# Block-causal attention and a gated MLP on one core: the smallest weights guarded by ScalarE, on-chip transfers issued by ScalarE, and half of w2 converted after the MLP has begun

## The chip, the cores and the metric

The kernel runs on one core of a Trainium2 chip. The metric is the device time of one execution in microseconds (us), as the median of three runs. Engines are named as the profile names them: PE is the matrix engine (PEld its weight loads), DVE the vector engine, ACT the scalar engine (ScalarE), POOL is GpSimd, SP the sync engine, which in the kernel before issues every DMA (transfer).

## The reference

Eight sequences of 576 tokens pass through attention with 8 heads of 64, causal by blocks of 64 tokens, and the 4608 results of 512 features through a gated MLP:

```python
scores = scale * np.matmul(q, k.transpose(0, 1, 3, 2))      # 8 x 8 x 576 x 576
scores = np.where(block_i >= block_j, scores, -1e9)
attn = np.exp(scores - max); attn = attn / (sum(attn) + 1e-9)
x = (attn @ v) as 4608 x 512
h = ((x @ w1) * (x @ w2)) @ w3                               # 512 -> 1024 -> 1024
out = h @ w_out                                              # 1024 -> 512
```

The weights come as 64-bit floats (w1, w2, w3, w_out), so the kernel reads each as pairs of 32-bit words and makes 32-bit floats of them on the chip.

## The kernel before, in words

**The folded weights.** The kernel multiplies w3 by w_out once, at the start (eight groups of matmuls at L358, 16 instructions each, in plain 32-bit floats), so that the MLP is only x@w1, x@w2, their product, and one matmul with the folded weight. For the rest each operand is kept as a rounded high part and a low part of the remainder (`w1h`, `w1l`, `wh`, `wl` and so on), and three matmuls stand for one.

**The early stage** runs pairs 0 to 3 of heads (the whole first sequence), one pair after the other (`pair(n)`), with `EARLY_PLAN` as the order of its steps. A letter is a step: S a tile of scores with its exponentials (L230, L238), V a part of the probabilities times v (L269), M a part of the next pair's row maxima (`shift_mask`), A and B the next operands of the scores (`prep_qk`), N and T taking and normalising the result, and C one step of the generator `gen_w`, which loads weights. There are ten Cs for a pair, so 40 in all, and `gen_w` has 40 steps: 8 for w_out, 24 for w3 (two loads for each of eight groups) with the eight loads of w1 between them, and 8 for w2, in the order of w2's rows c and then of its two column halves h.

**One load of a weight** (`load_w`, 40 of them, 128 x 512 values each) is a DMA of 512 KB into one of five buffers `wraw`, then on ACT the absolute value of the upper word (L135), then on DVE four operations: a maximum with 2^-15, the guard for tiny values (L136), a shift with a mask (L137), an operation that puts the sign in (L138), and one that puts the lower word in (L141). For w1 and w2 (`load_split`) a rounded copy on ACT (L147) and a subtraction on DVE (L148) follow.

**The two on-chip transfers.** `shift` (L196) moves the row maxima of one head into a row of the score operands, and `prep_qk` (L206) copies the high parts of q and k to the other half of the partitions. Both are issued by SP, behind the loads that SP issues in the same queue.

**The main stage** runs pairs 4 to 31 with `PLAN`; its letter F is one step of the MLP of the sequences already done (`gen_moe`): 6 matmuls, and four steps make one of eight column blocks f of x@w1 and x@w2. Block f uses the columns 128f to 128f+127 of w1 and w2. In pair 4 the first three Fs are left out (`DELAY`), so that its two halves j hold 9 and 12 of these steps. The order of PE is written out by hand from here on, by the order of the program (`manual_schedule`); on the other engines a scheduler orders instructions by their place in the program (their priority) and by when it expects them to be ready.

**Memory.** The early pool (w_out, w3, `ve`, `pe`, `wraw`, `wbits`) is closed after pair 3, and the late pool (`ph`, `rsum`, `pl`, `vs`, `gh`, `gl`, and then by first use `p32`, `xlow`, `a32`, `g32`, `xh`, `xl`, `o32`) takes the same addresses. A late buffer waits for the last reader of the early one under it.

Of the kernel before, what the change touches and what calls it, by code (L numbers as in the profile page):

```python
# [16 lines left out]
P = 128  # L17
B, H, S, D = 8, 8, 576, 64
BLK = 64
# [11 lines left out]
BIG = 8.0e9  # L31

# [18 lines left out]
)  # L51

# [6 lines left out]
def block_causal_attention__then__gated_mlp_kernel(ctx, tc, qkv, consts, ident_in, w1, w2, w3t, wout, out_t):  # L59
# [47 lines left out]
    def open_early(pool):  # L107
        tl["early"] = pool
        tl["wo"] = pool.tile([P, NF, DM], F32, name="wo")

    def open_late():
# [7 lines left out]
        tl["gh"] = pool.tile([P, NF, HALF], F32R, name="gh")  # L119
        tl["gl"] = pool.tile([P, NF, HALF], F32R, name="gl")  # L120

    def load_w(dst, src, k):
# [13 lines left out]
        V.tensor_scalar(out=u, in0=u, scalar1=2.0**-15, scalar2=None, op0=ALU.max)  # L136
# [13 lines left out]
    def load_rows(dst_h, dst_l, src, c):  # L150
        for h in range(2):
# [42 lines left out]
    def shift(n, j):  # L194
        row = qk[j][oth[j].start : oth[j].start + 1, 1, :].rearrange("p (i r) -> p i r", r=BLK)
        nc.sync.dma_start(out=row.bitcast(F32), in_=ms_of[n][0:NB, j * BLK : (j + 1) * BLK].bitcast(F32))  # L196

    def prep_qk(n, j):
# [7 lines left out]
        nc.sync.dma_start(out=qk[j][x, 0::2, :].bitcast(F32), in_=high.bitcast(F32))  # L206
# [15 lines left out]
    def s_tile(n, j, parts, p_early):  # L222
# [10 lines left out]
        for c, ks, at, q0, q1 in todo:  # L233
# [7 lines left out]
            if c == 0:  # L241
                p32 = rsum[:, q0:q1]
            else:
                p32 = tl["late"].tile([P, 448], F32, tag="p32", name=f"p{n}_{j}", bufs=2)[ks, 0:w]
# [91 lines left out]
    def gen_w(wp):  # L336
# [12 lines left out]
        for m in range(NF):  # L349
            t3 = wp.tile([P, NF, P], F32, tag="w3", name="w3", bufs=2)  # L350
# [16 lines left out]
        for c in range(NC):  # L367
            yield from load_rows(w2h, w2l, w2, c)

    def gen_moe(b):  # L370
        mp, gh, gl = tl["late"], tl["gh"], tl["gl"]
        for h in range(2):
            for f in range(NF):
# [11 lines left out]
                a32 = mp.tile([P, HALF], F32, tag="a32", name="a32", bufs=2)  # L385
                nc.scalar.copy(a32, acc[0][:, 0:HALF])
                g32 = mp.tile([P, HALF], F32, tag="g32", name="g32", bufs=2)
                nc.vector.tensor_tensor(out=g32, in0=acc[1][:, 0:HALF], in1=a32, op=ALU.mult)  # L388
                nc.scalar.copy(gh[:, f, :], g32)  # L389
                nc.gpsimd.tensor_tensor(out=gl[:, f, :], in0=g32, in1=gh[:, f, :], op=ALU.subtract)  # L390
                yield
            for e in range(DM // P):
                t = ps_m.tile([P, 512], F32, tag="psm", name="o")
                es = slice(e * P, (e + 1) * P)
                for f in range(NF):
                    for s, (l, r) in enumerate(((wh, gh), (wl, gh), (wh, gl))):
                        nc.tensor.matmul(t[:, 0:HALF], l[:, f, es], r[:, f, :], start=(f == 0 and s == 0), stop=(f == NF - 1 and s == 2))  # L397
# [23 lines left out]
    def pair(n):  # L421
# [9 lines left out]
        for j in range(2):  # L431
            xps = ps_x.tile([P, 1024], F32, tag="psx", name=f"x{n}_{j}")
            p_early = wp.tile([P, 1600], F32, tag="pe", name=f"pe{n}_{j}") if early else None
# [39 lines left out]

    for n in range(NPAIR):
        pair(n)
    fill(weights, 100)
# [60 lines left out]
```

## Time and profile before

| | |
|---|---|
| median of 3 runs | 1007.41 us (1006.82 to 1007.84) |
| the profiled execution's own time | 1008.37 us |
| its span, first to last instruction | 1006.6 us |
| PE busy | 961.6 us, 96% |
| DVE busy | 718.8 us, 71% |
| ACT busy | 547.9 us, 54% |
| POOL busy | 521.1 us, 52% |

The profile is one execution, recorded by the hardware. Busy times are sums over the whole span; the early stage is the first 150 us or so of it. The main stage is long and uniform, so the shares of the whole span say little of the early one, and the rows further down are cut by stretches.

### The profile page before, as it was taken

How to read it: one execution, taken by the hardware profiler on the slowest of the kernel's cores; microseconds unless marked ns; L12 is line 12 of the kernel's file. 1: busy time of each engine (PE TensorE's matmuls, PEld its weight loads, DVE VectorE, ACT ScalarE, POOL GpSimd, SP SyncE). 2: the span in 40 equal slices, each digit the busy share in tenths (PEclk: the TensorE clock that was granted, in tenths of full speed). 3: DMA queues.
4: the chain of work that ended last, by engine and by line, in shares of the span. 5: the costliest groups of instructions: out<-in, count | busy, mean ns of one | idle time of the engine just before them, and what ended most of it. 6: DMA issues, size and time to landing. Idle time of an engine off the chain costs nothing.

```text
span 1006.6 us, 18165 instructions
## 1 busy us (share of the span) xinstructions
PE 961.6 (96%) x6594; PEld 886.1 (88%) x6624; DVE 718.8 (71%) x1356; ACT 547.9 (54%) x1433; POOL 521.1 (52%) x525
## 2 busy tenths in 40 slices
PE   4699958999999999999999999999999999999998
PEld 2354548999999999999999999999999999999998
DVE  7999997767777777777777767777777777774100
ACT  4655755555565655555555566555555655653211
POOL 0000006667665766666666657576666766573211
PEclk9799978999999999999999999999999999999999
DMA  8776522122212221221222222212212222110000
GB/s 247 240 257 195 170 82 61 55 80 61 85 57 78 61 74 38 70 73 56 78 61 85 61 74 61 84 32 67 73 58 76 61 85 61 37 24 25 1 25 24
DMA packets 36409, 80.39 MB, mean 80 GB/s; under 512 B 4384, under 2 KB 20896, under 8 KB 36320
## 3 DMA queue, kind: packets, MB, share of 16 engines
q1 hardware_dynamic: 36320, 79.23, 26.5%
q8 instruction: 52, 0.85, 0.4%
q14 instruction: 37, 0.30, 0.1%
HBM read 50.76 MB, written 9.44 MB: 60 GB/s over the span
## 4 chain that ended last, share of the span: by engine, by line
PE 60%; DVE 23%; ACT 9%; issue 6%; DMA 2%; DVEq 0%; ACTq 0%
PE ab L381 23%; PE o L397 20%; DVE pl L248 7%; PE s L230 6%; PE x L285 4%; PE mx L179 3%; DVE g L388 2%; ACT ph L246 2%; PE w L358 2%; ACT p L245 2%; DVE m L183 2%; DVE wbits L138 1%; DVE x L323 1%; DVE rb L322 1%; DVE qk L157 1%
## 5 line engine op out<-in xcount | busy, mean ns | idle before, releaser
L251 POOL TENSOR_TENSOR rsum<-rsum,p 128x448 f32<-128x448 f32 x224 | 178.3, 796 | 120.4 <-ACT p L245 113.6
L248 DVE TENSOR_TENSOR pl<-p,ph 128x448 fp32r<-128x448 f32 x168 | 150.9, 911 | 64.1 <-ACT ph L246 63.2
L389 ACT CAST gh<-g 128x288 fp32r<-128x288 f32 x128 | 55.5, 433 | 219.3 <-DVE g L388 219.3
L390 POOL TENSOR_TENSOR gl<-g,gh 128x288 fp32r<-128x288 f32 x128 | 108.3, 846 | 123.0 <-ACT gh L389 122.9
L230 PE MATMUL s<-qk 128*128 128x288 f32 (+4 forms) x768 | 160.7, 317 | 9.2 <-DMA qk<-ms 3.5
L381 PE MATMUL ab<-xh,w1h 128*128 128x288 f32 x512 | 152.0, 297 | 6.8 <-ACT xh L332 6.8
L381 PE MATMUL ab<-xh,w2h 128*128 128x288 f32 x512 | 154.1, 301 | 0.0
L397 PE MATMUL o<-gh,wh 128*128 128x288 f32 x512 | 153.4, 300 | 0.0
L381 PE MATMUL ab<-xh,w1l 128*128 128x288 f32 x512 | 151.6, 296 | 0.0
L381 PE MATMUL ab<-xl,w2h 128*128 128x288 f32 x512 | 151.5, 296 | 0.0
L381 PE MATMUL ab<-xl,w1h 128*128 128x288 f32 x512 | 151.5, 296 | 0.0
L381 PE MATMUL ab<-xh,w2l 128*128 128x288 f32 x512 | 151.4, 296 | 0.0
L397 PE MATMUL o<-gl,wh 128*128 128x288 f32 x512 | 150.8, 295 | 0.0
L397 PE MATMUL o<-gh,wl 128*128 128x288 f32 x512 | 150.8, 295 | 0.0
L207 POOL TENSOR_TENSOR qk<-raw,qk 64x1152 fp32r<-64x1152 f32 x54 | 144.3, 2672 | 2.0
L220 POOL TENSOR_TENSOR vs<-raw,vs 128x320 fp32r<-128x320 f32 x56 | 49.9, 891 | 174.2 <-ACT vs L157 174.2
L230 PEld LDWEIGHTS s<-qk 128*128 128x128 f32 (+1 forms) x768 | 116.9, 184 | 26.1 <-issue 6.1
L183 DVE TENSOR_REDUCE m<-mx 128x1 f32<-128x512 f32 (+6 forms) x320 | 128.6, 449 | 15.8 <-PE mx L179 13.2
L246 ACT ACTIVATE ph<-s 128x288 fp32r<-128x288 f32 x336 | 131.3, 392 | 0.0
L388 DVE TENSOR_TENSOR g<-ab,a 128x288 f32<-128x288 f32 x128 | 57.7, 451 | 74.4 <-PE ab L381 71.2
L245 ACT ACTIVATE p<-s 128x448 f32<-128x448 f32 x224 | 85.5, 382 | 45.8 <-PE s L230 44.2
L285 PE MATMUL x<-ph,vs 128*128 128x128 f32 x336 | 104.1, 319 | 0.0
(71 smaller groups left out, 2141.6 us busy)
## 6 DMA issues: line engine op xcount, KB each, us to landing
raw<-in_qkv SPq DMA_DIRECT2D x32, 896.0 KB
qk<-qk SPq DMA_DIRECT2D x64, 288.0 KB
out_t<-o SPq DMA_DIRECT2D x64, 144.0 KB
wraw<-in_w3t SPq DMA_DIRECT2D x16, 512.0 KB
wraw<-in_w SPq DMA_DIRECT2D x16, 512.0 KB
wraw<-in_wout SPq DMA_DIRECT2D x8, 512.0 KB
qk<-ms SPq DMA_DIRECT2D x64, 2.2 KB
cst<-in_consts SPq DMA_DIRECT2D x1, 288.0 KB
```

What stands on the lines that cost most here:

```text
L183: nc.vector.reduce_max(m[:, col : col + 1], sc, axis=AX.X)
L207: (nc.vector if n <= EARLY else nc.gpsimd).tensor_tensor(out=low, in0=rqk[o], in1=high, op=ALU.subtract)
L230: nc.tensor.matmul(t[ks, at : at + q1 - q0], qk[j][:, 2 + s, kr], qk[j][:, s, q0:q1], start=(s == 0), stop=(s == 1))
L245: nc.scalar.activation(p32, t[ks, at : at + w], AF.Exp, scale=SCALE)
L246: nc.scalar.activation(ph[ks, o : o + w], t[ks, at : at + w], AF.Exp, scale=SCALE)
L248: nc.vector.tensor_tensor(out=low, in0=p32, in1=ph[ks, o : o + w], op=ALU.subtract)
L251: nc.gpsimd.tensor_tensor(out=r, in0=r, in1=p32, op=ALU.add)
L285: nc.tensor.matmul(xps[:, to : to + w], v[:, c, :], pr[:, a : a + w], start=(u < 2 and s == 0), stop=(u in (0, len(PV) - 1) and s == len(p ...
L381: nc.tensor.matmul(t[:, 0:HALF], l[:, c, fs], r, start=(c == 0 and s == 0), stop=(c == NC - 1 and s == 2))
L388: nc.vector.tensor_tensor(out=g32, in0=acc[1][:, 0:HALF], in1=a32, op=ALU.mult)
L390: nc.gpsimd.tensor_tensor(out=gl[:, f, :], in0=g32, in1=gh[:, f, :], op=ALU.subtract)
L397: nc.tensor.matmul(t[:, 0:HALF], l[:, f, es], r[:, f, :], start=(f == 0 and s == 0), stop=(f == NF - 1 and s == 2))
```

## The change

- `load_w`: for w_out and w3 (24 of the 40 loads) the guard is not DVE's maximum any more. ACT takes the upper 16 bits of each absolute value as an unsigned integer, subtracts 0x3800 by a bias and cuts at zero (Relu), in place. For w1 and w2 (16 loads) the maximum stays. `wbits` has 5 buffers instead of 6.
- `queue(n)`: the transfers of L196 and L206 of pairs 0 to 4 are issued by ACT, later ones by SP as before.
- w2 is loaded by column halves: first the four loads of columns 0 to 511, then the four of columns 512 to 1023. The last four Cs do nothing (`LEAVE`), and those four loads follow after pair 3, still before the early pool is closed. Pair 4's first half (j = 0) takes a priority as of before these loads.
- The late buffers are laid out by hand: `p32`, `a32` and `g32` are two plain buffers each, used in turn; `gh` and `gl` are two halves each (f 0 to 3 and f 4 to 7); the early `w3` stands right behind w_out; `pe` is 2048 columns wide, of which 1600 are used as before.

```diff
 def load_w(dst, src, k):
-        u = tl["early"].tile([P, 512], F32, tag="wbits", name="wbits", bufs=6)
+        u = tl["early"].tile([P, 512], F32, tag="wbits", name="wbits", bufs=5)
...
         nc.scalar.activation(u, high.bitcast(F32), AF.Abs)
-        V.tensor_scalar(out=u, in0=u, scalar1=2.0**-15, scalar2=None, op0=ALU.max)
+        if dst is None:
+            V.tensor_scalar(out=u, in0=u, scalar1=2.0**-15, scalar2=None, op0=ALU.max)
+        else:
+            top = u.bitcast(U16).rearrange("p (c two) -> p c two", two=2)[:, :, 1]
+            nc.scalar.activation(top, top, AF.Relu, bias=floor)
...
+    def queue(n):
+        return nc.scalar if n <= EARLY else nc.sync
...
-        nc.sync.dma_start(out=row.bitcast(F32), in_=ms_of[n][...])
+        queue(n).dma_start(out=row.bitcast(F32), in_=ms_of[n][...])
...
-        nc.sync.dma_start(out=qk[j][x, 0::2, :].bitcast(F32), in_=high.bitcast(F32))
+        queue(n).dma_start(out=qk[j][x, 0::2, :].bitcast(F32), in_=high.bitcast(F32))
...
-        for c in range(NC):
-            yield from load_rows(w2h, w2l, w2, c)
+        for h in range(2):
+            for c in range(NC):
+                yield from load_rows(w2h, w2l, w2, c, [h])
...
                 if step == "C":
-                    fill(weights, 1)
+                    if left[0] > LEAVE:
+                        left[0] -= 1
+                        fill(weights, 1)
                     continue
-                with tc.high_priority(offset=0) if early else nullcontext():
+                with (
+                    tc.high_priority(offset=0) if early
+                    else tc.high_priority(offset=tc.cur_priority - left[1]) if n == NPAIR and j == 0
+                    else nullcontext()
+                ):
...
+    left = [10 * NPAIR, 0]
     for n in range(NPAIR):
         pair(n)
+    left[1] = tc.cur_priority
     fill(weights, 100)
```

## Rows read from the trace of the kernel before

**Rows 1.** Busy time by stretches of the span. Columns: the stretch and its length in us, then PE, PEld, DVE, ACT and POOL busy us with the number of instructions, then the granted PE clock (1.00 is full speed), the busy share of the DMA engines and GB/s.

```profile
17.00:41.70 24.70, 15.31 (x59) 10.07 (x59) 23.60 (x50) 16.38 (x33) 0.00 (x0) 0.89 0.80 232
41.70:125.00 83.30, 81.80 (x250) 41.98 (x254) 81.78 (x172) 50.83 (x99) 0.00 (x0) 0.97 0.67 210
125.00:138.00 13.00, 11.78 (x51) 7.71 (x51) 12.03 (x22) 8.31 (x17) 0.00 (x0) 0.87 0.44 135
138.00:153.50 15.50, 3.82 (x16) 3.07 (x14) 14.28 (x29) 6.39 (x13) 2.52 (x2) 0.64 0.09 20
153.50:167.00 13.50, 13.49 (x78) 12.96 (x80) 9.48 (x15) 6.96 (x21) 8.47 (x8) 0.78 0.31 92
167.00:181.00 14.00, 14.00 (x109) 13.63 (x108) 11.60 (x27) 9.08 (x25) 9.58 (x10) 1.00 0.10 21
181.00:211.00 30.00, 29.71 (x221) 28.79 (x221) 21.29 (x39) 17.62 (x49) 18.79 (x19) 1.00 0.29 82
...
241.00:900.00 659.00, 654.61 (x4824) 635.26 (x4847) 489.18 (x909) 379.08 (x1046) 435.01 (x430) 1.00 0.22 64
```

**Rows 2.** PE's instructions in order of time: start, length (us), line, operation, number merged, and in brackets the idle time before them and what ended it.

```profile
41.76 9.58 PE L358 MATMUL w<-wo,w 128*128 128x512 f32 x16 [4.41 <-DVE w L141]
...
61.65 7.11 PE L358 MATMUL w<-wo,w 128*128 128x512 f32 x16
...
120.39 4.45 PE L358 MATMUL w<-wo,w 128*128 128x512 f32 x10
...
137.40 0.43 PE L269 MATMUL x<-pe,ve 64*128 64x64 f32 x2
...
143.43 1.09 PE L230 MATMUL s<-qk 128*128 128x288 f32 x3 [3.50 <-DMA qk<-ms]
...
153.50 0.61 PE L381 MATMUL ab<-xh,w1h 128*128 128x288 f32 x1 [6.82 <-ACT xh L332]
...
158.90 0.44 PE L381 MATMUL ab<-xh,w1h 128*128 128x288 f32 x1
...
159.51 0.29 PE L381 MATMUL ab<-xh,w1h 128*128 128x288 f32 x1
...
176.58 0.38 PE L381 MATMUL ab<-xh,w2h 128*128 128x288 f32 x1
```

**Rows 3.** The chain of waits that ended last, 112 to 154 us: start, length (us), and what the chain consists of there.

```profile
136.01 1.16 ACT qk L157
137.19 2.90 DMA qk<-qk
140.08 0.61 ACT w2h L147
...
145.46 0.35 DVE tr L309
...
150.75 0.57 DVE w2l L148
151.32 1.35 DVE x L323
153.02 0.44 ACT xh L332
```

**Rows 4.** DVE's instructions in order of time, columns as in Rows 2.

```profile
37.87 0.42 DVE L137 TENSOR_SCALAR wbits<-wbits 128x512 int32<-128x512 int32 x1
38.20 0.42 DVE L136 TENSOR_SCALAR wbits<-wbits 128x512 f32<-128x512 f32 x1
38.54 0.69 DVE L138 SCALAR_TENSOR_TENSOR wbits<-wraw,wbits 128x512 int32<-128x512 int32 x1
39.14 0.42 DVE L137 TENSOR_SCALAR wbits<-wbits 128x512 int32<-128x512 int32 x1
...
122.32 0.75 DVE L323 TENSOR_TENSOR x<-x,rb 128x576 f32<-128x576 f32 x1
...
145.46 0.78 DVE L309 STREAM_TRANSPOSE tr<-x 64x576 f32<-64x576 f32 x1
...
147.59 0.17 DVE L310 TENSOR_SCALAR rr<-tr 64x18 f32<-64x18 f32 x1
...
149.67 0.26 DVE L320 RECIPROCAL rr<-rr 128x18 f32<-128x18 f32 x1
149.97 0.78 DVE L322 STREAM_TRANSPOSE rb<-rr 128x576 f32<-128x576 f32 x1
```

**Rows 5.** Groups of instructions of the first 155 us: line, engine, operation, shapes, number, then busy us and mean ns of one, and the idle time before them.

```profile
L136 DVE TENSOR_SCALAR wbits<-wbits 128x512 f32<-128x512 f32 x40 | 16.5, 417 | 0.3 <-ACT wbits L135 0.3
...
L147 ACT CAST w2h<-wbits 128x512 fp32r<-128x512 f32 x8 | 4.9, 617 | 6.8 <-DVE wbits L141 6.8
```

**Rows 6.** The same view, the absolute value on ACT, and beside it two of them in order of time.

```profile
L135 ACT ACTIVATE wbits<-wraw 128x512 f32<-128x512 f32 x40 | 26.9, 677 | 19.0 <-DMA wraw<-in_w3t 9.4 <-DMA wraw<-in_w 4.9 <-DMA wraw<-in_wout 2.5
...
18.37 1.25 ACT L135 ACTIVATE wbits<-wraw 128x512 f32<-128x512 f32 x2
```

**Rows 7.** The two on-chip transfers in the first 155 or 160 us, as SP issues them (shortest, median and longest time of SP for one issue, in ns), and what SP's queue waited for: us in total, times, longest.

```profile
L196 SPq DMA_DIRECT2D qk<-ms x10: 751/794/887, 17.1 to 141.7; - x10
...
L206 SPq DMA_DIRECT2D qk<-qk x10: 602/660/687, 6.5 to 137.2; - x10
...
SPq L206 <- PE s L230: 9.1, 4, 4.0
```

More of the change, by code (lines that the diff above doesn't have):

```diff
@@ L31 @@
 BIG = 8.0e9
+U16 = mybir.dt.uint16
 PC = [0, 576, 1024, 1344, 1536]
@@ L51 @@
 )
+LEAVE = 4
 DELAY = 3
@@ L109, in open_early @@
         tl["wo"] = pool.tile([P, NF, DM], F32, name="wo")
+        tl["w3"] = [pool.tile([P, NF, P], F32, name=f"w3_{i}") for i in range(2)]
     def open_late():
@@ L118, in open_late, with late_tile @@
         tl["vs"] = [pool.tile([P, 5, P], F32R, name=f"vs{j}") for j in range(2)]
-        tl["gh"] = pool.tile([P, NF, HALF], F32R, name="gh")
-        tl["gl"] = pool.tile([P, NF, HALF], F32R, name="gl")
+        tl["p32"] = [pool.tile([P, 448], F32, name=f"p32_{i}") for i in range(2)]
+        tl["a32"] = [pool.tile([P, HALF], F32, name=f"a32_{i}") for i in range(2)]
+        tl["g32"] = [pool.tile([P, HALF], F32, name=f"g32_{i}") for i in range(2)]
+        g = [[pool.tile([P, NF // 2, HALF], F32R, name=f"g{p}{i}") for p in "hl"] for i in range(2)]
+        tl["gh"], tl["gl"] = zip(*g)
+    turn = {"p32": 0, "a32": 0, "g32": 0}
+    def late_tile(name):
+        turn[name] ^= 1
+        return tl[name][turn[name]]
+    floor = cpool.tile([P, 1], F32, name="floor")
+    nc.vector.memset(floor, -float(0x3800))
     def load_w(dst, src, k):
         t = tl["early"].tile([P, 1024], F32, tag="wraw", name="wraw", bufs=5)
-        u = tl["early"].tile([P, 512], F32, tag="wbits", name="wbits", bufs=6)
+        u = tl["early"].tile([P, 512], F32, tag="wbits", name="wbits", bufs=5)
         wide = t.bitcast(I32)
@@ L148, in load_split, with load_rows @@
         nc.vector.tensor_tensor(out=dst_l, in0=val, in1=dst_h, op=ALU.subtract)
-    def load_rows(dst_h, dst_l, src, c):
-        for h in range(2):
+    def load_rows(dst_h, dst_l, src, c, hs=range(2)):
+        for h in hs:
             cs = slice(h * 512, (h + 1) * 512)
@@ L195, in shift @@
         row = qk[j][oth[j].start : oth[j].start + 1, 1, :].rearrange("p (i r) -> p i r", r=BLK)
-        nc.sync.dma_start(out=row.bitcast(F32), in_=ms_of[n][0:NB, j * BLK : (j + 1) * BLK].bitcast(F32))
+        queue(n).dma_start(out=row.bitcast(F32), in_=ms_of[n][0:NB, j * BLK : (j + 1) * BLK].bitcast(F32))
     def prep_qk(n, j):
@@ L243, in s_tile @@
             else:
-                p32 = tl["late"].tile([P, 448], F32, tag="p32", name=f"p{n}_{j}", bufs=2)[ks, 0:w]
+                p32 = late_tile("p32")[ks, 0:w]
             nc.scalar.activation(p32, t[ks, at : at + w], AF.Exp, scale=SCALE)
@@ L366, in gen_w @@
             evacuate()
-        for c in range(NC):
-            yield from load_rows(w2h, w2l, w2, c)
+        for h in range(2):
+            for c in range(NC):
+                yield from load_rows(w2h, w2l, w2, c, [h])
     def gen_moe(b):
-        mp, gh, gl = tl["late"], tl["gh"], tl["gl"]
+        mp = tl["late"]
+        gh = [tl["gh"][f // 4][:, f % 4, :] for f in range(NF)]
+        gl = [tl["gl"][f // 4][:, f % 4, :] for f in range(NF)]
         for h in range(2):
@@ L384, in gen_moe @@
                     acc.append(t)
[L385 removed]
+                a32 = late_tile("a32")
                 nc.scalar.copy(a32, acc[0][:, 0:HALF])
[L387 removed]
+                g32 = late_tile("g32")
                 nc.vector.tensor_tensor(out=g32, in0=acc[1][:, 0:HALF], in1=a32, op=ALU.mult)
[L389 to L390 removed]
+                nc.scalar.copy(gh[f], g32)
+                nc.gpsimd.tensor_tensor(out=gl[f], in0=g32, in1=gh[f], op=ALU.subtract)
                 yield
@@ L396, in gen_moe @@
                     for s, (l, r) in enumerate(((wh, gh), (wl, gh), (wh, gl))):
-                        nc.tensor.matmul(t[:, 0:HALF], l[:, f, es], r[:, f, :], start=(f == 0 and s == 0), stop=(f == NF - 1 and s == 2))
+                        nc.tensor.matmul(t[:, 0:HALF], l[:, f, es], r[f], start=(f == 0 and s == 0), stop=(f == NF - 1 and s == 2))
                     if f % 2 and f < NF - 1:
```

4 lines of the change are left out of this document (2 added, 2 removed).

## The prediction

> **What bounds the kernel now.** I read the busy time by stretches first [rows 1]. From 241 to 900 us PE is busy 654.6 of 659 us at full clock and nothing else is near that: the main stage is PE's, and the change takes no matmul away. So what can be won lies before it. There the reader should look at PE and DVE side by side. From 17 to 41.7 us DVE is busy 23.6 of 24.7 us and PE 15.3. From 41.7 to 125 us both are full: PE 81.8 and DVE 81.8 of 83.3 us. From 138 to 153.5 us DVE is busy 14.3 of 15.5 us and PE 3.8, at a clock of 0.64.
>
> Busy could mean waiting, so PE's order of time comes next [rows 2]. Sixteen L358 instructions take 7.11 us at 61.65 and ten take 4.45 at 120.39, that is 0.44 us each throughout, so PE works there at one steady rate. Two other things stand in these rows. The first group starts late, after 4.41 us of idling for DVE, and takes 9.58 us, which is the rate of the lower clock (1.2 GHz). And the last probabilities-times-v of pair 3 ends at 137.8 us, while the MLP gets its operand only at 153.5, after 6.82 us of idling.
>
> The chain of waits says what lies between: work on w2 (L147, L148), with the transpose of pair 3's result at 145.46 and its normalising at 149.97 and 151.32 strung in between [rows 3, 4]. DVE takes its instructions in a fixed order, and w2's operations stand ahead of the result. So the bounds in order are: DVE to 41.7 us, PE with DVE beside it to 125, DVE alone to 153.5, then PE.
>
> **The guard.** Durations overlap on DVE: a shift starts 0.33 us and a maximum 0.34 us before the next instruction, though each is listed at 0.42; an operation of two inputs costs 0.60 [rows 4]. I count by these distances. 24 maxima at 0.34 are 8.2 us of DVE. How many lie on the path? Ten come before the first L358 (eight loads of w_out, two of w3), 3.4 us, in the stretch where DVE is the bound. The others fall between 41.7 and 125 us, where PE is full without them, so they shorten nothing by themselves. Bounds of the first part are 0 (the DMA engines are busy 0.80 of that stretch [rows 1], so the weights may not come sooner) and 3.4 us. I take 3.4, since PE's wait named DVE and not a transfer.
>
> On ACT 24 instructions are new. The nearest row is the absolute value of the same 512 columns: 677 ns, the second of two 0.58 us after the first [rows 6], so 13.9 to 16.2 us. Bounds: all of it hidden, since ACT is busy only 75.5 of the 121 us from 17 to 138 [rows 1], or as much on the path as rival D says. I take it as hidden but for the friction below.
>
> The row says that ACT needs 677 ns where DVE needs 417 [rows 5, 6]. A rule of the Trainium skill speaks against the move: the page "ScalarE: Activation LUTs", section "Rules for kernel authors", says to use VectorE and not ScalarE for relu and max, and its section on the table load gives 280 ns + 0.833 ns per column with a bias pointer, an estimate of 707 ns and 17.0 us for the 24. The rows agree with its direction; it speaks of the price of one instruction, and by it rival D would have 0.8 us more to place.
>
> **Transfers by ACT.** SP needs 794 ns for one issue of L196 and 660 for one of L206, and there are ten of each in pairs 0 to 4 [rows 7]: 14.5 us that move to ACT's queue. No row shows an issue by ACT. The bounds are nothing and SP's own price, and I take SP's price for ACT's time. Behind a waiting issue ACT's exponentials would stand, and PE's V steps wait for these. But the copy of L206 follows ACT's own cast, which overwrites the same operands and so has waited for the same matmuls; L196 follows ACT's own product. What the transfers may win is SP's delay behind its loads, of which I take nothing. The fifth buffer instead of a sixth `wbits`, the halved `gh` and `gl` and the buffers used in turn issue nothing more; I take zero for them.
>
> **The second half of w2.** One such load costs DVE 2 x 0.34 + 3 x 0.60 = 2.48 us with its subtraction, and four cost 9.9 us. These leave the stretch before 153.5 us. Then DVE alone would be done by 153.5 - 8.2 - 9.9 = 135.4 us. PE alone: the last V ends at 137.8 - 3.4 = 134.4 us, and behind it come transpose (0.78), the sums (0.17 and 0.26), the second transpose (0.78), the product (0.75) and the cast on ACT (0.44) in a row [rows 3, 4], 3.2 us, with some 0.4 us of hand-overs: 138.0 us. So with w2 out of the way PE and this last run of short steps are late next, and PE decides. The two bounds lie only 2.6 us apart, and ACT is fuller. For the friction I take 1.5 us, what PE idles from 41.7 to 125 us where two engines are full; its bounds are 0 and 8 (the remaining tail as it is). The MLP's first operand is then there at 139.5 us instead of 153.5: **14.0 us won.**
>
> **What the second half costs later.** It is used first by block f = 4, in step 19 of pair 4's 21 MLP steps, which began at 176.58 us, 23 us after the stage began [rows 2]. DVE is busy 9.48 + 11.60 = 21.1 of pair 4's 27.5 us and 21.3 of the next 30 [rows 1], so it has 6.4 us free in pair 4, and some 1.5 us while pair 3's last run waits. 9.9 - 6.4 - 1.5 = 2.0 us don't fit and hold PE. Bounds are 0 (the 8.7 us free in the next pair take them) and 9.9. Behind these operations DVE's low parts of the probabilities are queued, and PE's V steps wait for them. `xlow` of pair 4 lies over a raw buffer of the second moved load; two loads are 5.0 us of DVE and its first half has 4.0 free, so I add nothing.
>
> **The clock.** After its idling PE runs at 1.2 GHz until about 159.2 us (0.44 us for an instruction at 158.90, 0.29 at 159.51 [rows 2]), which costs half of 5.7, so 2.9 us. It may be kept or lost a second time; I take no change, with 2.9 us on either side.
>
> **The sum.** 14.0 - 2.0 = 12.0 us less. The profiled execution's 1008.37 us (span 1006.6 and 1.8 around it) becomes 996.4. That execution is 0.96 us above the median of the runs; against 1007.41 the same step gives **995.4 us**.
>
> **Rivals.**
>
> A. The forecast, 990 to 1001 us: chance 0.60.
>
> B. More than that: DVE sets the end at 135.4 us (18.1 us), nothing spills, and PE keeps its clock (2.9 us), 21 us in all: 986 us. For it: PE's idling of 3.50 and 6.82 us before 153.5 goes. Against it: PE needs its 138.0 us. Chance 0.10, for 986 to 990 and a little below.
>
> C. The gain is hidden: the last stretch is a run of hand-overs rather than DVE's amount. Pair 4's scores wait there for a cast of 1.16 us, a transfer of 2.90 us, and L196 until 143.43 [rows 2, 3], and none of that gets shorter. If only the 3.4 us of the start and the moved operations after 145.46 on the chain (0.57 at 150.75, and some 2 us between) are won, 6 us, and 2 to 4 are given back later, the time is 1004 us, with 1001 to 1006.5 as its stretch. For it: the DMA step on the chain; against it: pair 3's result waited from 137.8 to 145.46 with nothing but w2 and the masks on DVE. Chance 0.20, of which 0.06 falls within 0.2% of the time before.
>
> D. ACT takes over as the bound (the slower side). It gets 16.2 us of guard, 14.5 of issues, and, if the 9.1 us for which SP's copies waited for PE's scores [rows 7] now stop ACT, 39.8 us; less 4 x (0.68 + 0.62) = 5.2 us moved away with w2 that is 34.6 us. Its place is ACT's queue from 17 to 138 us, where exponentials stand behind each wait. ACT has 45.5 us free there, mostly in waits that can't all be filled. From 35% on the path (12.0 of 34.6) the gain is gone; at 60% it is 20.8 us, and the time 1007.4 + 20.8 - 12.0 = 1016 us. For it: ACT's queue is in order and would be some 90% full. Against it: nothing on the chain before waits long for ACT. Chance 0.10, of which 0.02 falls within 0.2%.
>
> **How the numbers follow.** What a measurement of this kernel can tell from no change is about 0.2%, 2 us. Faster by more: A 0.60, B 0.10 and 0.14 of C, so 0.84; within: 0.06 + 0.02 = 0.08; slower: 0.08. The range is 986 to 1006 us: it holds A, B but for its lowest part and most of C, and leaves out D and the slow end of C.
>
> **What would show it.** The first L358 starts near 38 us instead of 41.76; if not, the loads held it. The first L381 that waits for `xh` starts near 139.5 us, and no w2 operation stands between pair 3's last V and its L323. ACT is 82 to 91% busy from 17 us up to there; if PE comes to wait for `pe` or `qd` by more than a few us in all, D is at work. From then to the end PE needs what it needed before, 1006.6 - 153.5 = 853.1 us, and some 2 more, with the wait in pair 4 at L285 or at block f = 4. A stage start later than 147 us, or a spill over 8 us, makes the forecast wrong.

## The result, and the profile after

The changed kernel is **slower**: 1014.98 us (median of 6 runs, 1010.75 to 1017.26) against 1007.51 (6 runs, 1004.62 to 1008.05), a ratio of 1.0076, 95% interval 1.0061 to 1.0090. The forecast was 995.4, with a range up to 1006. The profiled execution took 1017.09 us, its span is 1015.3. A profile is a single execution: this one lies 2.1 us above its kernel's median, that of the kernel before 1.0 us, so differences of a microsecond or two between profiles may be scatter.

Busy time by stretches after, with the columns of [rows 1]:

```profile
17.00:41.70 24.70, 16.95 (x56) 10.56 (x57) 20.34 (x42) 19.97 (x39) 0.00 (x0) 0.86 0.72 217
41.70:125.00 83.30, 78.14 (x243) 40.23 (x242) 74.00 (x145) 58.10 (x108) 0.00 (x0) 0.96 0.64 200
125.00:138.00 13.00, 11.46 (x42) 6.80 (x40) 12.86 (x22) 9.90 (x20) 0.00 (x0) 0.92 0.47 140
138.00:153.50 15.50, 9.48 (x38) 6.75 (x36) 14.91 (x34) 9.09 (x19) 0.00 (x0) 0.72 0.20 66
...
167.00:181.00 14.00, 13.85 (x83) 13.41 (x84) 7.61 (x16) 6.73 (x19) 5.43 (x6) 0.77 0.00 1
...
241.00:900.00 659.00, 654.86 (x4838) 636.60 (x4837) 487.32 (x904) 380.45 (x1050) 433.39 (x429) 1.00 0.23 65
```

DVE did get lighter: by 3.3 us from 17 to 41.7 and by 7.8 from there to 125. But PE got emptier beside it (78.14 us instead of 81.80 from 41.7 to 125), and from 138 to 153.5 DVE is as full as before. The stretch from 241 to 900 is what it was. So the loss lies before 181 us.

PE in order of time after (columns of [rows 2]; L384, L295, L256, L410 and L311 are L358, L269, L230, L381 and L285 of before; the first line shows 12 of the group's 16 instructions):

```profile
40.78 5.42 PE L384 MATMUL w<-wo,w 128*128 128x512 f32 x12
...
125.95 3.59 PE L384 MATMUL w<-wo,w 128*128 128x512 f32 x8
...
146.35 1.00 PE L295 MATMUL x<-pe,ve 128*128 128x192 f32 x2 [1.77 <-ACT pe L264]
148.03 0.68 PE L295 MATMUL x<-pe,ve 64*128 64x64 f32 x2 [0.67 <-ACT pe L264]
...
156.19 0.61 PE L410 MATMUL ab<-xh,w1h 128*128 128x288 f32 x1 [4.13 <-ACT xh L358]
...
157.25 1.48 PE L256 MATMUL s<-qk 128*128 128x448 f32 x4
...
167.15 0.53 PE L311 MATMUL x<-pl,vs 128*128 128x192 f32 x1 [2.81 <-DVE pl L274]
```

The fold starts 1.0 us earlier and ends 4.7 us later (129.5 instead of 124.8). Pair 3's last V ends 10.9 us later, at 148.7. The tail behind it is shorter, and the matmul that waits for the MLP's operand starts at 156.19 instead of 153.50: 2.7 us late. From there to the end PE needs 859.1 us instead of 853.1: another 6.0. The two make up the 8.7 us between the spans.

DVE in order of time after, which answers to [rows 4] (L170 is the subtraction of L148, L349 the product of L323):

```profile
150.98 0.78 DVE L335 STREAM_TRANSPOSE tr<-x 64x576 f32<-64x576 f32 x1
151.79 0.69 DVE L170 TENSOR_TENSOR w2l<-wbits,w2h 128x512 fp32r<-128x512 f32 x1
152.51 0.17 DVE L336 TENSOR_SCALAR rr<-tr 64x18 f32<-64x18 f32 x1
152.72 0.69 DVE L170 TENSOR_TENSOR w2l<-wbits,w2h 128x512 fp32r<-128x512 f32 x1
153.33 0.26 DVE L346 RECIPROCAL rr<-rr 128x18 f32<-128x18 f32 x1
153.50 0.63 DVE L170 TENSOR_TENSOR w2l<-wbits,w2h 128x512 fp32r<-128x512 f32 x1
154.05 0.77 DVE L348 STREAM_TRANSPOSE rb<-rr 128x576 f32<-128x576 f32 x1
154.92 0.76 DVE L349 TENSOR_TENSOR x<-x,rb 128x576 f32<-128x576 f32 x1
```

In after **the second half of w2 did not leave**. In the program its loads stand behind pair 3, but the last of its subtractions still run between the transpose of pair 3's result and its normalising, as before. All eight loads of w2 are done before the MLP's waiting matmul. E1, E2, E8 and E16 below show that this isn't so in every kernel with this place in the program.

The guard, in groups from 17 to 156 us (columns: operation, count, busy us, mean ns, then idle time before them and what ended it), against [rows 5, 6]:

```profile
L153 ACT ACTIVATE wbits<-wraw 128x512 f32<-128x512 f32 x37 | 24.1, 670 | 14.4 <-DMA wraw<-in_w3t 9.3 <-DMA wraw<-in_w 2.2 <-DVE wbits L163 2.1
L158 ACT ACTIVATE wbits<-wbits,floor 128x512 uint16<-128x512 uint16 x22 | 18.6, 868 | 0.2
L159 DVE TENSOR_SCALAR wbits<-wbits 128x512 int32<-128x512 int32 x38 | 15.6, 421 | 5.7 <-ACT wbits L158 5.6
```

One guard takes ACT 868 ns, and DVE's shift waits for it 5.6 us in all.

The transfers, on ACT in order of time (for [rows 7]):

```profile
145.12 0.60 ACTq L232 DMA_DIRECT2D qk<-qk  x1
...
146.12 1.59 ACTq L222 DMA_DIRECT2D qk<-ms  x2
147.76 0.22 ACT L264 ACTIVATE pe<-s 64x64 f32<-64x64 f32 x1 [1.46 <-issue]
```

Two issues of 0.8 us stand in front of the exponential for which PE's last V of pair 3 waits. In all ACT's waits for its own issues are 2.6 us from 17 to 156 us (1.5 for `pe`, 0.8 for `qd`, 0.3 for an absolute value).

### The profile page after: what moved, and what is told of

The parts are those of the page before. It is cut to its first block, busy times and chain, and to the rows that moved or that the text cites. A ratio compares the mean times of both kernels' runs of the same rounds, so it can differ in the third digit from the quotient of the medians.

```text
span 1015.3 us, 18193 instructions
## 1 busy us (share of the span) xinstructions
PE 968.0 (95%) x6624; PEld 892.5 (88%) x6624; DVE 710.8 (70%) x1333; ACT 565.1 (56%) x1457; POOL 519.7 (51%) x525
## 4 chain that ended last, share of the span: by engine, by line
PE 59%; DVE 23%; ACT 10%; issue 6%; DMA 3%; POOL 0%; DVEq 0%; ACTq 0%; POOLq 0%; SPq 0%
PE ab L410 22%; PE o L426 20%; DVE pl L274 7%; PE s L256 6%; PE x L311 4%; PE mx L205 3%; DVE g L417 3%; ACT ph L272 2%; ACT p L271 2%; DMA wraw<-in_w3t 2%; DVE x L349 2%; PE w L384 2%; DVE rb L348 1%; DVE m L209 1%; ACT xh L358 1%
## 5 line engine op out<-in xcount | busy, mean ns | idle before, releaser
L277 POOL TENSOR_TENSOR rsum<-rsum,p 128x448 f32<-128x448 f32 x224 | 177.8, 794 | 120.2 <-ACT p L271 113.5
L419 POOL TENSOR_TENSOR gl<-g,gh 128x288 fp32r<-128x288 f32 x128 | 108.4, 847 | 127.3 <-ACT gh L418 127.3
L256 PE MATMUL s<-qk 128*128 128x288 f32 (+4 forms) x768 | 162.6, 319 | 6.4 <-ACT pe L264 3.9
L410 PE MATMUL ab<-xh,w1h 128*128 128x288 f32 x512 | 152.8, 298 | 4.1 <-ACT xh L358 4.1
L410 PE MATMUL ab<-xh,w2h 128*128 128x288 f32 x512 | 155.1, 303 | 0.0
L410 PE MATMUL ab<-xl,w1h 128*128 128x288 f32 x512 | 152.6, 298 | 0.0
L410 PE MATMUL ab<-xh,w1l 128*128 128x288 f32 x512 | 152.4, 298 | 0.0
L410 PE MATMUL ab<-xh,w2l 128*128 128x288 f32 x512 | 152.3, 297 | 0.0
L410 PE MATMUL ab<-xl,w2h 128*128 128x288 f32 x512 | 152.3, 297 | 0.0
L233 POOL TENSOR_TENSOR qk<-raw,qk 64x1152 fp32r<-64x1152 f32 x54 | 144.2, 2670 | 2.0
L256 PEld LDWEIGHTS s<-qk 128*128 128x128 f32 (+1 forms) x768 | 118.4, 186 | 20.6 <-ACT pe L264 5.8
L311 PE MATMUL x<-ph,vs 128*128 128x128 f32 x336 | 104.3, 320 | 0.0
```

The source lines that it names most:

```text
L233: (nc.vector if n <= EARLY else nc.gpsimd).tensor_tensor(out=low, in0=rqk[o], in1=high, op=ALU.subtract)
L256: nc.tensor.matmul(t[ks, at : at + q1 - q0], qk[j][:, 2 + s, kr], qk[j][:, s, q0:q1], start=(s == 0), stop=(s == 1))
L277: nc.gpsimd.tensor_tensor(out=r, in0=r, in1=p32, op=ALU.add)
L311: nc.tensor.matmul(xps[:, to : to + w], v[:, c, :], pr[:, a : a + w], start=(u < 2 and s == 0), stop=(u in (0, len(PV) - 1) and s == len(p ...
L410: nc.tensor.matmul(t[:, 0:HALF], l[:, c, fs], r, start=(c == 0 and s == 0), stop=(c == NC - 1 and s == 2))
L419: nc.gpsimd.tensor_tensor(out=gl[f], in0=g32, in1=gh[f], op=ALU.subtract)
```

## The experiments

The kernel before had medians of 1006.96 to 1007.26 us beside the experiments, and the ratios are to these. "After" and "before" name the two kernels. No experiment leaves out a part of the reference.

**Undoing one part of the change**

E1, the guard back on DVE:

```diff
-        if dst is None:
-            V.tensor_scalar(out=u, in0=u, scalar1=2.0**-15, scalar2=None, op0=ALU.max)
-        else:
...
-            nc.scalar.activation(top, top, AF.Relu, bias=floor)
+        V.tensor_scalar(out=u, in0=u, scalar1=2.0**-15, scalar2=None, op0=ALU.max)
```

> The changed kernel with the guard of all 40 loads back on DVE; transfers by ACT, w2 by halves and the laid-out late buffers stay. Theory G (the guard on ACT is the loss: 24 of them took 20.2 us there, 0.87 us each, and DVE stood 5.6 us in its order waiting for them): DVE takes 8.2 us more work but stops waiting, ACT loses 20 us, and the time falls from about 1015 to 1008 or below. Theory T (ACT's queue is held by the transfers): little changes, 1012 to 1016 us. Theory W (the order of w2, the priority and the late buffers do it, in pair 4, where PE stood 2.8 us for the low part of the probabilities and ran on at the lower clock): 1012 us or more, with the same idling in pair 4.

Measured: 1016.91 us, ratio 1.0092 [1.0075, 1.0109]. The guard is not what costs.

E2, the transfers back on SP:

```diff
-        return nc.scalar if n <= EARLY else nc.sync
+        return nc.sync
```

> The changed kernel with all transfers issued by SP again; guard on ACT, w2 by halves and late buffers stay. G: 1013 to 1017 us, as the changed kernel. T: ACT loses 20 issues of 0.66 to 0.79 us each, its exponentials of pair 3 no longer wait (one stood 1.46 us behind two issues at 146 us), and the time falls to about 1008. W: 1013 to 1017 us with the idling in pair 4 as it was.

Measured: 1011.56 us, 1.0041 [1.0026, 1.0056]: 3.4 us come back. Pair 3's last V ends at 138.8 us, near the 137.8 of before.

E3, w2 by rows as before, with no Cs left out and no priority for pair 4:

```diff
-LEAVE = 4
+LEAVE = 0
...
-                    else tc.high_priority(offset=tc.cur_priority - left[1]) if n == NPAIR and j == 0
...
-        for h in range(2):
-            for c in range(NC):
-                yield from load_rows(w2h, w2l, w2, c, [h])
+        for c in range(NC):
+            yield from load_rows(w2h, w2l, w2, c)
```

> The changed kernel with w2 by rows again, all forty steps taken within pairs 0 to 3, and no early priority for pair 4; guard on ACT, transfers by ACT and the laid-out buffers stay. All eight loads of w2 were converted before the first waiting matmul of the MLP in the changed kernel too (last subtraction at 153.5 us, that matmul at 156.2), so by every theory the start of the main stage moves by less than 2 us. G and T: 1012 to 1017 us. W: pair 4 loses its 2.8 us of idling for DVE and the lower clock behind it, and the time falls by 4 to 6 us to about 1009.

Measured: 1010.32 us, 1.0031 [1.0018, 1.0044]. This takes 4.7 us out; E8 says which of its edits does most of that.

E8, after without the priority of pair 4's first half:

```diff
-                    else tc.high_priority(offset=tc.cur_priority - left[1]) if n == NPAIR and j == 0
```

> The changed kernel without the early priority of pair 4's first half, all else as changed. Theory P (each step of that half starts at one and the same priority, so that the sums were put ahead of the last low part on DVE, which then waited for POOL and held PE 2.8 us, with PE at the lower clock after it): the order on DVE in pair 4 is that of the kernel before, the idling for it is under 0.5 us, and the time is about 1010 to 1011 us, as with w2 by rows. Rival (the halves of w2 hold pair 4): it stays at 1013 to 1016 us.

Measured: 1011.19 us, 1.0035 [1.0021, 1.0050]: 3.8 us less. In its profile pair 4's next scores start at 156.45 us, in after at 157.25, and from there to the end it takes 854.2 us instead of 858.1. PE's wait for `pl` is gone: the three kernels with the priority (after, E1, E2) have it, with 2.2 to 2.8 us, and E3, E8 and E16 do not. So the priority is what the main stage lost. What PE waits for at 156.45 is not the MLP's operand, which is there at 147.8 us, but pair 4's exponentials:

```profile
156.45 1.65 PE L256 MATMUL s<-qk 128*128 128x448 f32 x4 [6.45 <-ACT ph L272]
```

How the priority costs, the order on DVE shows. After:

```profile
164.34 0.78 DVE L324 TRANSPOSE_TENSOR_REDUCE part<-rsum 128x18 f32<-128x576 f32 x1 [1.05 <-POOL rsum L277]
165.05 2.05 DVE L274 TENSOR_TENSOR pl<-p,ph 128x192 fp32r<-128x192 f32 x1
```

E8:

```profile
163.58 0.75 DVE L274 TENSOR_TENSOR pl<-p,ph 128x192 fp32r<-128x192 f32 x1
...
165.23 0.77 DVE L324 TRANSPOSE_TENSOR_REDUCE part<-rsum 128x18 f32<-128x576 f32 x1
```

With the priority every step of pair 4's first half begins again at one and the same priority. The sums, a later step, come ahead of the last low part, wait for POOL, and the low part then takes 2.05 us instead of 0.75, while POOL works on the operands of the next scores. PE idles 2.81 us for it and stands at a clock of 0.77 from 167 to 181 us, where it had 1.00 [rows 1]: some 3.2 us of 14.

E16, after with both of these undone (transfers by SP, no priority): the edits of E2 and E8.

> The changed kernel with SP's transfers and without the early priority: what stays is the guard on ACT, w2 by halves, and the layout. If the parts add up (the transfers gave back 3.4 us, the priority 3.8), 1007 to 1009 us. If they overlap, 1010 us or more.

Measured: 1007.00 us, 1.0002 [0.9991, 1.0014]. These two parts are the whole loss, and what is left of the change gains nothing. That is not for want of moved work: here the second half of w2 did leave. DVE, PE and ACT of E16 in order of time:

```profile
140.65 0.75 DVE L349 TENSOR_TENSOR x<-x,rb 128x576 f32<-128x576 f32 x1
141.31 0.68 DVE L170 TENSOR_TENSOR w2l<-wbits,w2h 128x512 fp32r<-128x512 f32 x1
...
144.53 0.69 DVE L170 TENSOR_TENSOR w2l<-wbits,w2h 128x512 fp32r<-128x512 f32 x1
...
147.57 0.69 DVE L170 TENSOR_TENSOR w2l<-wbits,w2h 128x512 fp32r<-128x512 f32 x1
...
150.28 0.69 DVE L170 TENSOR_TENSOR w2l<-wbits,w2h 128x512 fp32r<-128x512 f32 x1 [0.68 <-ACT w2h L169]
```

```profile
146.31 0.44 PE L410 MATMUL ab<-xh,w1h 128*128 128x288 f32 x1
...
151.62 1.65 PE L256 MATMUL s<-qk 128*128 128x448 f32 x4 [4.39 <-ACT ph L272]
```

```profile
141.43 0.77 ACT L358 CAST xh<-x 128x288 fp32r<-128x288 f32 x2
...
149.63 0.62 ACT L169 CAST w2h<-wbits 128x512 fp32r<-128x512 f32 x1 [3.16 <-DVE wbits L163]
...
151.17 0.40 ACT L272 ACTIVATE ph<-s 128x288 fp32r<-128x288 f32 x1
```

All four subtractions of the second half come behind the product that ends pair 3's normalising. The operand is there at 141.9 us, 11.6 sooner than before, and the matmul that waited for it in before (153.50) runs at 146.31 without waiting. But ACT has w2's copies ahead of pair 4's first exponentials, and the copies wait for DVE. So PE idles 4.39 us, and the next scores start at 151.62 us; in before it was

```profile
154.57 1.65 PE L230 MATMUL s<-qk 128*128 128x448 f32 x4
```

Of 11.6 us at the operand 3.0 are left there. E1 and E2 have all four subtractions behind the product too, and E8 three of them; the table behind E9 has their times.

**Adding one part to before**

E4, the guard alone: the lines of the change in `load_w`.

```diff
+            nc.scalar.activation(top, top, AF.Relu, bias=floor)
```

> The kernel before with the guard of w_out and w3 on ACT alone, nothing else. G: DVE waits for ACT, PE's folding matmuls end 4 to 5 us later than in the kernel before, and the time is 1010 to 1015 us. T and W: 8.2 us less on DVE shortens the last stretch before the main stage, and the time is 1000 to 1005 us.

Measured: 1005.96 us, 0.9990 [0.9980, 0.9999], a gain that can hardly be told from none. The fold's first matmul starts at 42.77 us (before 41.76) and its last ends at 124.84, to the hundredth as before.

E5, the transfers alone:

```diff
-        nc.sync.dma_start(out=row.bitcast(F32), in_=ms_of[n][...])
+        queue(n).dma_start(out=row.bitcast(F32), in_=ms_of[n][...])
...
-        nc.sync.dma_start(out=qk[j][x, 0::2, :].bitcast(F32), in_=high.bitcast(F32))
+        queue(n).dma_start(out=qk[j][x, 0::2, :].bitcast(F32), in_=high.bitcast(F32))
```

> The kernel before with the transfers of pairs 0 to 4 issued by ACT, nothing else. Theory T (ACT's queue is held by them; taking them out of the changed kernel gave 3.4 us back): 1010 to 1011 us, with pair 3's last probabilities-times-v 3 to 8 us later than the 137.8 us of the kernel before, behind exponentials that wait for issues. Rival (the transfers cost only beside the guard, which fills ACT too): 1006 to 1008 us.

Measured: 1010.27 us, 1.0039 [1.0027, 1.0052]. The same cost as in after.

E7, the layout of the late buffers alone (after without guard, transfers, order of w2 and priority): the edits of E1, E2 and E3 together.

> The changed kernel with guard, transfers, the order of w2 and the priority undone: what stays is the laid-out late buffers and the fifth buffer instead of a sixth. If the layout is neutral: 1006 to 1009 us and pair 4 as in the kernel before. If the layout itself holds pair 4 (or the smaller number of buffers holds the loads): 1010 us or more.

Measured: 1008.38 us, 1.0010 [1.0000, 1.0021]: at most a microsecond or two.

**What the transfers cost**

E10 moves only the copies of L206 to ACT, E11 only the maxima of L196, E17 moves both to POOL, which is idle up to 148 us in before:

```diff
-        nc.sync.dma_start(out=qk[j][x, 0::2, :].bitcast(F32), in_=high.bitcast(F32))
+        (nc.scalar if n <= EARLY else nc.sync).dma_start(out=qk[j][x, 0::2, :].bitcast(F32), in_=high.bitcast(F32))
```

```diff
-        nc.sync.dma_start(out=row.bitcast(F32), in_=ms_of[n][...])
+        (nc.scalar if n <= EARLY else nc.sync).dma_start(out=row.bitcast(F32), in_=ms_of[n][...])
```

```diff
+        return nc.gpsimd if n <= EARLY else nc.sync
```

> The kernel before with only the copies of L206 issued by ACT; the row maxima of L196 stay with SP. If the cost of ACT's transfers (3.3 us with both) is one issue's time on ACT, ten of twenty issues make about half of it: 1008 to 1009 us. If it comes from the pairs of L196 that stand one behind the other ahead of an exponential, this kernel costs nothing: 1006 to 1007.5 us. If it comes from the other order that the scheduler works out for ACT and DVE, either half may cost all of it, 1010 us.

> The other half: only the row maxima of L196 issued by ACT. By time of issue 1008 to 1009 us; by the pairs of L196 1009 to 1010.5 us; by the order, either 1007 or 1010 us, and then the order of DVE's instructions between 118 and 150 us is that of the kernel with both.

> The kernel before with the transfers of pairs 0 to 4 issued by POOL, which is idle then. Theory T in its plain form (time of issue on ACT, or ACT standing in order behind a transfer's wait): no cost, 1005.5 to 1008 us. Theory O (another engine's issue changes the order that the scheduler works out, and that costs): 1009 us or more, or another order that happens to be better, 1005 us or less, with hundreds of lines of difference in DVE's order as in the kernel with ACT's copies.

Measured: E10 1011.72 us, 1.0041 [1.0028, 1.0054]; E11 1009.01 us, 1.0020 [1.0010, 1.0030]; E17 1011.14 us, 1.0047 [1.0028, 1.0065]. E17 settles one thing: on an engine with nothing behind the issues they cost as much. So the cost does not need issue time on ACT.

What the kernels with their transfers off SP share is seen in SP's queue: the weights come later. SP's last nine loads of w1 and w2 in after (start, length up to the end of the last one, number):

```profile
99.89 30.88 SPq L148 DMA_DIRECT2D wraw<-in_w  x9
```

and the last three in E2, which differs by the transfers alone:

```profile
116.64 0.34 SPq L148 DMA_DIRECT2D wraw<-in_w  x1
119.72 3.46 SPq L148 DMA_DIRECT2D wraw<-in_w  x2
```

The last load is issued at 130.8 us there and at 123.2 here. The pairs, each differing by transfers alone, with ACT's waits for weights from 17 to 156 us:

| pair: by SP, then elsewhere | last load issued, us | ACT waits for weights, us | ratio |
|---|---|---|---|
| before, E11 | 126.4, 127.3 | 14.3, 18.6 | 1, 1.0020 |
| before, E5 | 126.4, 127.7 | 14.3, 22.1 | 1, 1.0039 |
| before, E10 | 126.4, 133.0 | 14.3, 23.6 | 1, 1.0041 |
| before, E17 | 126.4, 130.9 | 14.3, 24.6 | 1, 1.0047 |
| E2, after | 123.2, 130.8 | 4.6, 11.5 | 1.0041, 1.0076 |
| E16, E8 | 121.8, 128.2 | 4.8, 14.8 | 1.0002, 1.0035 |

After and E5 issue the last nine loads in a row, and what SP waits for before them is DVE, which has to give a buffer free. E11's profile is of an execution of 1004.25 us, 4.8 below its median, so its row can't show its cost. The table points at the order of DVE's work on the weights.

E15 changes an order alone, by two letters of the early plan:

```diff
-"M S S S C S C C C C M S V V B C M M V A V M V M Q B M A B M N"
+"M S S S C S C C C C M S V V B M C M V A V M V M Q B M A B M N"
```

> The kernel before with two neighbouring letters of the early plan exchanged (a C and the M behind it), so the same instructions with other places in the program: 118 lines of difference in DVE's order and 37 in ACT's. If the order that the scheduler works out is by itself worth microseconds (theory O), the time is off the kernel before by 2 us or more, one way or the other; if not, it is within 1.5 us of 1007.1.

Measured: 1007.87 us, 1.0006 [0.9994, 1.0018], no difference, though the last load is issued at 130.7 us and ACT waits 16.1 us for weights. So a late load alone is not dear. That the transfers' place costs 0.2 to 0.5% is shown, in six pairs; that weights and order are how, is argued from the table and not shown. Another way stays open too: whether the moved transfers themselves land later from another queue was not measured.

**What the second half of w2 is worth when it is held**

E9 starts from E16 and makes the last four loads depend on pair 3's result: their absolute value adds a bias of zero that is computed from it. They get a lower priority than pair 4.

```diff
+            nc.scalar.activation(u, high.bitcast(F32), AF.Abs, bias=none)
...
+                            nc.vector.tensor_scalar(out=none, in0=x32[:, 0:1], scalar1=0.0, scalar2=None, op0=ALU.mult)
...
-    fill(weights, 100)
+    late_w[0] = True
+    with tc.high_priority(offset=-600):
+        fill(weights, 100)
```

> The changed kernel with SP's transfers and without the early priority, and the four loads of w2's second half held back in fact: their absolute values take a bias of zero that is worked out from pair 3's normalised result, and they stand at a lower priority. So DVE has no operation of theirs before that result. Theory H (w2 on DVE ahead of pair 3's result is what keeps the MLP from starting): the first matmul of the MLP that waits for its operand starts at 138 to 143 us, 9.9 us of DVE fall into pair 4, and the time is 996 to 1003 us. Rival L (the stretch before the main stage is a run of hand-overs that w2 only fills): that matmul starts at 147 us or later and the time is 1005 us or more. Rival S (what is won is paid back in pair 4): an early start, and PE idles in pair 4 by what was won, 1004 to 1010 us.

Measured: 1006.35 us, 0.9992 [0.9979, 1.0005]. ACT of E9 in order of time:

```profile
138.86 0.76 ACT L363 CAST xh<-x 128x288 fp32r<-128x288 f32 x2
139.53 2.75 ACT L156 ACTIVATE wbits<-wraw,none 128x512 f32<-128x512 f32 x4
...
150.00 0.62 ACT L174 CAST w2h<-wbits 128x512 fp32r<-128x512 f32 x1 [1.65 <-DVE wbits L168]
150.53 0.81 ACT L184 CAST vs<-raw 128x320 fp32r<-128x320 f32 x2
151.25 0.40 ACT L276 ACTIVATE rsum<-s 128x288 f32<-128x288 f32 x1
```

and PE:

```profile
141.62 0.44 PE L415 MATMUL ab<-xh,w1h 128*128 128x288 f32 x1
...
143.98 0.29 PE L415 MATMUL ab<-xl,w1h 128*128 128x288 f32 x1
152.00 1.65 PE L261 MATMUL s<-qk 128*128 128x448 f32 x4 [7.72 <-ACT ph L277]
```

The operand is there at 139.3 us (138.86 and a first cast of 0.44). Then ACT's order has four absolute values and four rounded copies, which wait 5.9 us for DVE, ahead of pair 4's first exponentials, and PE idles 7.72 us for these. PE comes to the matmul at which before waited until 153.50 at 143.72 us, and to the next scores at 152.00, where before it was 154.57. Most of what was won at the operand is given back at once.

The kernels side by side, from their profiles, in us (`xh` is the MLP's operand, `ph` pair 4's first exponentials; the next scores are the four instructions at 154.57 in before):

| kernel | pair 3's last V ends | `xh` is there | w2's subtractions behind pair 3's product | PE's wait for `ph` | next scores start | from there to the end |
|---|---|---|---|---|---|---|
| before | 137.8 | 153.5 | 0 | none | 154.57 | 852.0 |
| after | 148.7 | 156.1 | 0 | none | 157.25 | 858.1 |
| E1 | 145.0 | 150.4 | 4 | 4.91 | 157.04 | 857.8 |
| E8 | 142.4 | 147.8 | 3 | 6.45 | 156.45 | 854.2 |
| E2 | 138.8 | 143.4 | 4 | 2.91 | 152.49 | 857.3 |
| E16 | 137.3 | 141.9 | 4 | 4.39 | 151.62 | 852.7 |
| E9 | 134.7 | 139.3 | 4 | 7.72 | 152.00 | 850.8 |

Where the second half left, `xh` no longer decides when pair 4's scores start. E2 and after differ by the transfers alone: with the transfers on ACT pair 3's last V is 9.9 us later (E8 against E16: 5.1), and w2's subtractions stand ahead of its product.

E13 puts the four loads into pair 4's own order, as eight of half the size with buffers of their own, and gives the early subtractions to POOL; E14 is E13 with the early subtractions on DVE. Both have SP's transfers and no priority.

```diff
+LATE_PLAN = (
+    "B F B F S F S B F F S S F F F S W W M M V F W V V V F W R F F V Q N",
+    "M A S S A F F S W F M M W S F F F S W M A M W V V V F V F F V N Q F R T M F F",
+)
...
-        nc.vector.tensor_tensor(out=dst_l, in0=val, in1=dst_h, op=ALU.subtract)
+        nc.gpsimd.tensor_tensor(out=dst_l, in0=val, in1=dst_h, op=ALU.subtract)
```

```diff
-        nc.gpsimd.tensor_tensor(out=dst_l, in0=val, in1=dst_h, op=ALU.subtract)
+        (nc.vector if t is None else nc.gpsimd).tensor_tensor(out=dst_l, in0=val, in1=dst_h, op=ALU.subtract)
```

> The changed kernel with SP's transfers, without the early priority, with all subtractions of w1 and w2 on POOL, and with the second half of w2 loaded and converted within pair 4, as eight loads of 256 columns into buffers of their own, spread between pair 4's steps (their guard on ACT as well). DVE has 12.3 us less before pair 3's result. Theory H with the waiting moved as the held kernel showed it (there the operand was ready at 139.3 us, but ACT had four casts of w2 ahead of pair 4's first exponentials, and PE stood 7.7 us): here only two small casts can stand there, so PE's wait before pair 4 is under 4 us and the time 997 to 1002 us. Rival S (paid back in pair 4): PE idles there by 5 us or more in all and the time is 1004 us or more.

> The late-loaded kernel with the subtractions of the twelve early loads back on DVE (the four late ones stay on POOL). In the held kernel pair 3's result was ready at 138.8 us; with POOL's subtractions the late-loaded one was 7 us later than that. If POOL's subtractions were what slowed its early stage, the first matmul of the MLP starts at 140 to 144 us here and the time is 1003 to 1008 us, with pair 4 still giving back some 5 us; if late loading itself slows the early stage, it starts at 148 us or later and the time is 1012 us or more.

Measured: E13 1015.79 us, 1.0080 [1.0065, 1.0095]; E14 1008.57 us, 1.0008 [0.9994, 1.0022]. E14 starts the MLP at 146.55 us (before: 144.32), passes the matmul at which before waited until 153.50 at 148.71, without a wait, and starts the next scores at 149.43, 5.1 us sooner than before. But PE idles 5.4 us from 153.5 to 181 us, three waits of 1.2 us among them: no gain again. So the work of the second half is paid for in pair 4 as well, and the copies ahead of the exponentials are not the only place for it. The 7.2 us between E13 and E14 are POOL's.

E12 had asked for these alone: E4 with the subtractions of w1 and w2 on POOL.

```diff
-        nc.vector.tensor_tensor(out=dst_l, in0=val, in1=dst_h, op=ALU.subtract)
+        nc.gpsimd.tensor_tensor(out=dst_l, in0=val, in1=dst_h, op=ALU.subtract)
```

> The kernel before with the guard of w_out and w3 on ACT and the 16 subtractions of w1 and w2 (L148) on POOL, which is idle up to 150 us. DVE has 9.6 us less. Theory H (DVE's operations on w2 keep the MLP from starting): pair 3's result is normalised 4 to 8 us sooner than in the kernel with the guard alone (where its matmul started at 149.06 us), and the time is 999 to 1003 us. Rival (hand-overs set that stretch, POOL's slower subtraction is one more): 1004 to 1008 us.

Measured: 1009.29 us, 1.0021 [1.0010, 1.0033], 3.3 us more than E4, with 16 subtractions fewer on DVE. Groups of E12 from 17 to 156 us:

```profile
L156 POOL TENSOR_TENSOR w2l<-wbits,w2h 128x512 fp32r<-128x512 f32 x8 | 12.2, 1522 | 27.7 <-ACT w2h L155 27.7
L149 DVE SCALAR_TENSOR_TENSOR w<-wraw,wbits 128x512 int32<-128x512 int32 x16 | 11.9, 752 | 0.1
L141 DVE TENSOR_SCALAR wbits<-wbits 128x512 f32<-128x512 f32 x16 | 8.5, 534 | 0.4 <-ACT wbits L139 0.4
```

Each subtraction takes POOL 1522 ns, where DVE needs 677 in E4 by the same view, and DVE's own operations get longer beside it: 534 ns for the maximum (415 in E4), 752 for the last of the four (680 in E4).

## Why the prediction was wrong

**What bounds the kernel** held: the main stage is PE's at full clock (654.86 us of 659, 654.61 in [rows 1]), and all that was lost was lost before 181 us.

**The second half of w2, "14.0 us won", is the step that failed.** It took the lead of the MLP's operand for time won. In E2, E9 and E16 the second half does stand behind pair 3's result, and the operand comes at 143.4, 139.3 and 141.9 us; the forecast "with w2 out of the way" was 139.5. But PE has another wait right behind it: 2.91 to 7.72 us for pair 4's exponentials, which ACT's order has behind w2's copies. The next scores start only 2.1 to 3.0 us sooner than before. By the medians 0.3 us (E16) and 0.6 (E9) are left, no more than noise. "PE alone" was too short as well: its 138.0 us leaves out that pair 4's scores stand in front, which waited for L196's transfer until 143.43 [rows 2], and nine matmuls of the MLP behind them. PE came to the waiting matmul at 146.7 us in before and idled 6.82 there, so an operand at 139.5 by itself could win 6.8 us and not 14.0.

In after itself not even the operand's lead was there. "These leave the stretch before 153.5 us" did not come true, as pair 3's last V came 10.9 us later than before and the last subtractions of the four loads stood ahead of its normalising. E2, with the transfers back on SP, has the lead. No data dependence holds the loads back in either kernel; the order of the engines decides, why the scheduler made it so is not shown, and the forecast had no rival for that.

The payment behind it was mis-sized and put on the wrong engine. 2.0 us were set for DVE in pair 4. In E9 and E16 PE idles behind ACT, in E14 by 5.4 us in pair 4.

**The priority was not priced at all.** The diff shows that each step of pair 4's first half starts again at one priority; that the steps need then no longer keep the order of the program on DVE and ACT could be read from it. It costs 3.8 us by medians (E8).

**The transfers, of which the sum had nothing, cost 3.3 to 3.9 us** (E5, E17, and E2 from the other side). My bounds counted issue time on ACT, of which only 2.6 us turned into waits there, and looked for the trouble behind a waiting issue. POOL, with nothing to hold up, pays the same. The term that was missing is what moving the issues does to the order and timing of everything else; how it comes to 3 to 4 us stays open.

**The guard.** "I take 3.4" of the bounds 0 and 3.4 was wrong: the fold's first matmul came 1.0 us earlier in after, but there the transfers had moved too. The guard alone made it later: 42.77 us in E4 against 41.76, and 40.78 in after against 39.66 in E1. PE's wait named DVE's last operation, but by the program a chain stands in front of it, transfer, absolute value, guard, shift, and the guard moved from DVE's part of it to ACT's, where it takes longer. The 677 ns taken for ACT measured 868, so 20.8 us for 24 instead of at most 16.2. The Trainium skill's "ScalarE: Activation LUTs", in the section on the table load, would make it 707 ns, an estimate that the trace does not bear out either; the page's advice, in "Rules for kernel authors", to leave relu and max with VectorE fits the longer time. That the other 14 maxima shorten nothing was right for the fold: in E4 it ends where it did.

**Rival D** gave 1016 us and after took 1014.98, but not by its mechanism. For it speaks that PE waited 9.0 us for `pe` (5.1 and 3.9, by PE's waits from 17 to 156 us), where before it was 2.4. Against it speaks that taking the guard's 20.8 us off ACT gains nothing (E1), and that the transfers cost as much on POOL (E17). **Rival C** comes nearest to E2, E9 and E16: the gain is hidden by hand-overs, and PE's wait for the row maxima's transfer is still 2.2 to 3.0 us there. But the hand-over that hides most, w2's copies ahead of the exponentials on ACT, was not among those that it named, and its 6 us were not won.

**The clock** went the bad way of its 2.9 us (and the 9.58 us of the fold's first group are the lower clock's only in part: it was granted 0.50 from 41.8 to 45 us and 1.00 from 48 on): where before PE was at full speed from about 159.5 us on, in after it falls again with the idle time at 164 to 167, and 167 to 181 runs at 0.77.

The parts, by ratio from before: guard 0.9990, layout 1.0010, transfers 1.0039; and undone in after, transfers and priority give back 3.4 and 3.8 us. Without these two the kernel is back at 1.0002 (E16). No version beat the kernel before clearly; the nearest were E4, by 0.1%, and E9.

## What to carry to other kernels

The lead of one operand is not yet time won: before a gain is booked, look for what the engine waits for next. In E9 the operand came 14.2 us sooner and the next scores 2.6. Whoever moves work should follow it through every engine that it uses, since the four loads were booked on DVE and stood in ACT's order before the exponentials. A place in the program does not settle where a scheduler puts work on the engine either: the same place had w2 behind pair 3's result in E2 and ahead of it in after. An edit that only moves an issue or a priority costs nothing on paper, and cost 0.3 to 0.5% here each, so it is measured by itself.

## What had not been expected of the hardware

- ACT takes 868 ns for 512 unsigned 16-bit values that lie 4 bytes apart, in place with a bias from a buffer, and 670 for the absolute value of 512 32-bit words without one.
- DVE beside POOL: the same subtraction of 128 x 192 took 0.75 us in E8 and 2.05 in after, where POOL worked on a long operation (L233, 164.28 to 166.88 us, by POOL's order of time). In after, E1 and E2 (2.05 to 2.07) it ends 0.2 us behind that operation. POOL's being busy is not enough for it: in E8 POOL worked too, on the sums (L277, 163.43 to 164.50). Operations on the weights went from 415 to 534 ns and from 680 to 752 where POOL had the subtractions (E4, E12). In these profiles some work given to POOL was not free for DVE.
